# Keys and values dealt to partitions in pairs: the same loads in runs of 768 B instead of 1,536 B

## The chip, the cores and the metric

The kernel runs on one core of a Trainium2 chip. The metric is device time in microseconds (us) of one execution, lower is better. Five engines work beside each other and meet only through semaphores: TensorE (PE in the profile; PEld is its weight load), VectorE (DVE), ScalarE (ACT), GpSimd (POOL) and SyncE (SP). SP computes nothing here; it issues all DMAs, and 16 DMA engines carry them out.

## The reference

Attention over a cache of keys and values, with the projections of the queries and of the output. B = 8 batches, 112 queries each, D = 640; H = 32 heads of 192; 512 keys a head. Everything is bf16.

```python
q = transpose((x @ wq).reshape(B, Sq, H, Dh), 0, 2, 1, 3)
scores = einsum("bhqd,bhkd->bhqk", q, k_cache) * (Dh ** -0.5)
p = softmax(scores, axis=-1)
o = einsum("bhqk,bhkd->bhqd", p, v_cache)
return transpose(o, 0, 2, 1, 3).reshape(B, Sq, H * Dh) @ wo
```

The sum over the keys does not care in which order the 512 keys of a head stand, as long as keys, scores and values use the same order. That is the freedom which the change uses.

## The kernel before

**Tiling.** The 32 heads are four groups r of 8. A load i covers one group and one batch, r = i // 8, b = i % 8: K i and V i each hold 8 heads x 512 keys x 192, 1.573 MB. Each load serves two steps n = 2i and 2i + 1, with four heads each (`qd` = n % 2). For a step there are, in this order: the scores (`Sm`, `St`, L635 to L650), the softmax (`smax` on DVE L663, `exp` on ACT L668, `norm` on DVE L672), the transposes of p (`PT`, L706), and the value matmuls (`PVt` L739, `PVm` L750). Beside the steps run the query projection (`Q`, L590), which needs wq loads (`WQ`), and the output projection (`O`, L772), which needs wo loads (`WO`).

**How keys lie.** A head's 512 keys are dealt to 128 partitions, four neighbouring keys to each: partition r has keys 4r to 4r + 3, a run of 4 x 192 x 2 B = 1,536 B in memory. With q = 2a + e, a the pair and e the key in the pair, a run is (a, e, d). The 384 numbers of a pair make three blocks m of 128 after a transpose: block 0 is the first 128 of key e = 0, block 2 the last 128 of key e = 1, and block 1 holds the last 64 of the one and the first 64 of the other. A score bank therefore has 256 columns for a head and an e, those of a = 0 and a = 1; `QJ` = [0, 2, 1, 3] translates the order (e, a) of the score columns to the order (a, e) in which V's rows lie.

**How keys arrive.** The K loads 7 to 31 (`load_k`, L138) are transposing DMAs straight into `kt`, which has four buffers. The first seven loads (`load_kn`, L171, called KN 0 to 6; KN 0 in two halves) arrive plainly into borrowed space (`vt`, `wo_sb` or `accT` in the profile's names), are transposed by PE (`k_transposes`, L561) and moved to `kt` by ACT and DVE (L572). The values (`load_v`, L149) are plain loads into three buffers `vt`. At the end five p's (57 to 61) are transposed by DMA too (`TD`, L690).

**What sets the order.** Nothing is scheduled at run time. `ORDER_PE`, `ORDER_ACT`, `ORDER_DVE` and `ORDER_SP` are lists written out in the code, and every engine goes through its own list, waiting for semaphores. SP issues, in the order of `ORDER_SP`, a load as soon as the buffer is free (`deps`: for a K load the last score matmuls of the load four before, for a V load the last value matmuls of the load three before) and everything behind it in the list waits with it. Around the places that the prediction uses, the lists read:

```python
("K", 10), ("K", 9), ("V", 8), ("K", 11), ("WQ", 2, 0, 1), ("V", 9), ("V", 10), ...          # SP
("WQ", 3, 2, 1), ("V", 19), ("WQ", 3, 3, 1), ("WO", 2), ("V", 21), ("V", 22), ("K", 23), ...    # SP
("PT", 39, 5), ("Q", 6, 2, 0, 4), ("PVt", 38, 0), ("PVm", 38), ("PVt", 39, 5), ("Q", 6, 3, 0, 4), ("PVm", 39), ("S", 42),  # PE
```

Of the kernel before, what the change touches and what calls it, by code (L numbers as in the profile page):

```python
# [5 lines left out]
BF16 = mybir.dt.bfloat16  # L6
# [5 lines left out]
class Plan:  # L12
# [7 lines left out]
    def add(self, eng, name, deps, emit, sem=None, inc=1):  # L20
        assert name not in self.ops, name
        self.ops[name] = dict(eng=eng, deps=deps, emit=emit, sem=sem or eng, inc=inc)
# [30 lines left out]
def build_mha_kernel(nc, x, k_cache, v_cache, wq, wo, out):  # L53
    B, SQ, D = x.shape
# [3 lines left out]
    HU = 8  # L58
# [8 lines left out]
    KS, VS, QS = 4, 3, 2 * LP  # L67
# [18 lines left out]
    with ExitStack() as es:  # L86
        def sb(name, shape, dt):
            return es.enter_context(nc.sbuf_tensor(name, shape, dt))
# [2 lines left out]
        wo_sb = sb("wo_sb", [128, KB, D], BF16)  # L91
        accT = sb("accT", [128, 2, DC, SG], F32)
        xT_sb = sb("xT_sb", [128, DC, B * SQ], BF16)
        kt = sb("kt", [128, KS, 2, 3, HU * 128], BF16)
        vt = sb("vt", [128, VS, HU, 768], BF16)
        qr = sb("qr", [128, QS, 3, SG], BF16)
        qh = sb("qh", [128, 2, 2, 4, SQ], BF16)
# [9 lines left out]
        ps = es.enter_context(nc.psum_tensor("ps", [128, 8, 512], F32))  # L107
        psb = ps[:].bitcast(BF16)
# [4 lines left out]
        kn = [vt[:, VS - 1]]  # L113
# [5 lines left out]
        q_flat = qr[:].rearrange("p l c s -> p (l c s)")  # L119
        late = [wq_flat[:, i * 16 * SQ:(i + 1) * 16 * SQ] for i in range(4)] + [q_flat[:, 0:16 * SQ]]  # L120
        pT_late = dict(zip(BY_DMA, late))
        k3_flat = kt[:, KS - 1].rearrange("p a m c -> p (a m c)")
        zeros = k3_flat[:, 4 * D:4 * D + 256]
        xn = [k3_flat[:, 0:4 * D], acc_flat[:, 0:3 * D]]
        xn = [v.rearrange("p (c d) -> p c d", d=D) for v in xn]
# [7 lines left out]
        def load_k(i):  # L133
            r, b = divmod(i, B)
            name = ("K", i)

            def emit(e):
                src = k_cache[b, r * HU:(r + 1) * HU].rearrange("u (r q) d -> (u r) (q d)", q=4)  # L138
                return e.dma_start_transpose(kt[:, i % KS].rearrange("p a m c -> p (a m) c"), src)
            deps = [("St", 2 * (i - KS) + 1, 3)] if i >= KS else []  # L140
            if i == KS - 1:
                deps = [("XT", c) for c in range(4)]
            add("SP", name, deps, emit, f"mK{i % KS}", 16)

        def load_v(i):
            r, b = divmod(i, B)

            def emit(e):
                src = v_cache[b, r * HU:(r + 1) * HU].rearrange("u (r q) d -> r u (q d)", q=4)  # L149
                return e.dma_start(vt[:, i % VS], src)  # L150
            deps = [("PVm", 2 * (i - VS) + j, 1) for j in range(2)] if i >= VS else []
            if i == VS - 1:
                deps = [("KT", 0, p) for p in range(LP)]
            add("SP", ("V", i), deps, emit, f"mV{i % VS}", 16)
# [13 lines left out]
        def load_kn(i, lo, hi):  # L168

            def emit(e):  # L170
                return e.dma_start(kn[i][:, lo:hi, :], k_cache[i, lo:hi].rearrange("u (r q) d -> r u (q d)", q=4))  # L171
            old = [("KT", i - 2, p) for p in range(lo // 2, hi // 2)] if i > 2 else []
            add("SP", ("KN", i, lo, hi - lo), old, emit, f"mKN{i}_{lo}", 16)
            kn_of.update({(i, u): ("KN", i, lo, hi - lo) for u in range(lo, hi)})
# [382 lines left out]
        def k_transposes(i, p, bank, engs):  # L557
            def emit(e):
                for x in range(12):
                    c, u = divmod(x, 2)  # L560
                    ends = [e.transpose(psb[:, bank + t, x * 64:(x + 1) * 64],  # L561
                                        kn[i][64 * t:64 * t + 64, 2 * p + u, c * 128:(c + 1) * 128],
                                        ident[64 * t:64 * t + 64, 64 * t:64 * t + 64]) for t in range(2)]
                return tuple(ends)

            add("PE", ("KT", i, p), [kn_of[i, 2 * p], kn_of[i, 2 * p + 1]], emit, ("PE", "PE2"))
            old = [("St", 2 * (i - KS) + 1, 3)] if i >= KS else [("XT", x) for x in range(4)] if i == KS - 1 else []
            for t in range(2):
                def evac(e, t=t):
                    dst = kt[:, i % KS].rearrange("p a m (u t s) -> p (a m) u t s", t=2, s=64)[:, :, 2 * p:2 * p + 2, t, :]  # L570
                    src = psb[:, bank + t, 0:768].rearrange("p (c u s) -> p c u s", c=6, u=2)
                    return e.activation(dst, src, ACTF.Copy) if engs[t] == "ACT" else e.tensor_copy(dst, src)  # L572
                add(engs[t], ("evK", i, p, t), [("KT", i, p)] + old, evac)

# [27 lines left out]
        def q_of(n):  # L602

            r, b, qd = place(n)
            i, bb = q_slot(group(n), 2 * qd), b % (B // 2)
            return qr[:, i:i + 2, :, bb * SQ:(bb + 1) * SQ]
# [11 lines left out]
        def scores(n):  # L618
            qd = n % 2
            ktb = kt[:, n // 2 % KS]  # L620
            qv = q_of(n)

            def raw(j, c):
                return qv[:, j, c, :]

            def cs(i):
                return slice((4 * qd + i) * 128, (4 * qd + i + 1) * 128)

            for j in range(2):
                def emit(e, j=j):  # L630
                    for h in range(2):
                        i = 2 * j + h
                        ev, od = (raw(j, 0), qh[:, n % 2, j, 1, :]) if h == 0 else (qh[:, n % 2, j, 2, :], raw(j, 2))
                        hs = slice(h * 256, (h + 1) * 256)
                        e.matmul(ps[0:SQ, 2 * j, hs], ev, ktb[:, :, 0, cs(i)], start=(h == 0), stop=False,  # L635
                                 skip_group_check=True)
                        mm = e.matmul(ps[0:SQ, 2 * j + 1, hs], od, ktb[:, :, 2, cs(i)], start=(h == 0), stop=False,  # L637
                                      skip_group_check=True)
                    return mm
                add("PE", ("Sm", n, j), [("qc", n), ("smax", n - 1, 2 * j), ("smax", n - 1, 2 * j + 1)] +  # L640
                    ([("evK", n // 2, 2 * qd + i, t) for i in range(2) for t in range(2)] if n // 2 < NPL else [("K", n // 2)]), emit)
            for i in range(4):
                def emit(e, i=i):
                    j, h = divmod(i, 2)
                    ev, od = ((raw(j, 1)[0:64], qh[64:128, n % 2, j, 0, :]) if h == 0 else
                              (qh[0:64, n % 2, j, 3, :], raw(j, 1)[64:128]))
                    hs = slice(h * 256, (h + 1) * 256)
                    m1 = e.matmul(ps[0:SQ, 2 * j, hs], ev, ktb[0:64, :, 1, cs(i)], start=False, stop=True,  # L648
                                  skip_group_check=True)
                    m2 = e.matmul(ps[0:SQ, 2 * j + 1, hs], od, ktb[64:128, :, 1, cs(i)], start=False, stop=True,  # L650
                                  skip_group_check=True)
                    return m1, m2
                add("PE", ("St", n, i), [], emit, ("PE", "PE2"))
# [348 lines left out]
def bass_standalone__mha_block_cached__near_ridge_kernel(  # L1002
    nc: bass.Bass,
    x: bass.AP,
    k_cache: bass.AP,
    v_cache: bass.AP,
    wq: bass.AP,
    wo: bass.AP,
    out: bass.AP,
):  # L1010
    return build_mha_kernel(nc, x, k_cache, v_cache, wq, wo, out)
# [28 lines left out]
```

## Time and profile before

| | |
|---|---|
| median of 3 runs | 443.35 us (443.0 to 444.06) |
| profiled execution | span 444.4 us; no other time of it is given |
| granted TensorE clock, mean | 0.996 |
| busy | PE 96%, DVE 82%, ACT 78% of the span |
| DMA | 122.02 MB, mean 275 GB/s |
| V load, issue to landing | 9.0 us median, 32 of them |
| transposing K load, issue to landing | 10.2 us median, 25 of them |

The profile is that of one execution. A chain of work is followed back from the last instruction, at each step to what released it; its shares say which engine or transfer set the end. The window view gives busy time by engine, the granted clock, the mean busy share of the 16 DMA engines (over 1 where packets of one engine overlap) and what they moved. "Issue to landing" holds the time that a load stands behind others in the queue.

### The profile page before, as it was taken

The numbers are of one execution on the slowest core, as the hardware profiler recorded it, in microseconds if no ns is written. First come the engines' busy times: TensorE is split into PE (matmuls) and PEld (weight loads), VectorE is DVE, ScalarE is ACT, GpSimd is POOL, SyncE is SP. The second block draws the span as 40 slices with busy tenths as digits, with TensorE's granted clock in tenths as the row PEclk, the third lists the DMA queues.
The fourth block names the chain that finished last, engine by engine and source line by source line (L and its number), as shares of the span: only waits on it lengthen the run. The fifth ranks groups of instructions, "written<-read, shape, count | busy, mean of one in ns | idle before, by whom it ended". The sixth has DMA issues, their size and how long they took to land.

```text
span 444.4 us, 16108 instructions
## 1 busy us (share of the span) xinstructions
PE 425.1 (96%) x6805; PEld 304.5 (69%) x6805; DVE 363.2 (82%) x1165; ACT 344.4 (78%) x770; POOL 0.7 (0%) x6
## 2 busy tenths in 40 slices
PE   6998989889999999999899999999999999899995
PEld 4666666666677667777677766767667766676895
DVE  1579999879699889888989798889799888969871
ACT  3699999887678687978869688788778758965773
POOL 0000000000000000000000000000000000000000
PEclk9999999999999999999999999999999999989999
DMA  8999999998999999999999999999999999999952
GB/s 278 373 337 323 347 299 285 226 342 276 232 289 317 215 270 270 365 247 288 238 223 324 301 236 267 360 370 234 234 266 313 256 267 371 234 173 242 237 176 80
DMA packets 222184, 122.02 MB, mean 275 GB/s; under 512 B 164640, under 2 KB 222112, under 8 KB 222112
## 3 DMA queue, kind: packets, MB, share of 16 engines
q1 hardware_dynamic: 222112, 120.99, 106.6%
q8 instruction: 54, 0.88, 0.8%
q14 instruction: 18, 0.15, 0.1%
HBM read 78.22 MB, written 1.15 MB: 179 GB/s over the span
## 4 chain that ended last, share of the span: by engine, by line
PE 84%; DVE 5%; ACT 5%; DMA 4%; issue 2%; SPq 0%; ACTq 0%
PE ps L772 19%; PE ps L590 18%; PE ps L750 12%; PE ps L648 7%; PE ps L739 7%; PE ps L635 6%; PE ps L637 6%; PE ps L706 5%; DVE s_sb L663 3%; DMA wo_sb<-in_k_cache_dram 2%; PE ps L561 2%; ACT p_sb L668 2%; DMA wq_sb<-in_wq_dram 2%; ACT qr L595 1%; DVE p_sb L672 1%
## 5 line engine op out<-in xcount | busy, mean ns | idle before, releaser
L668 ACT ACTIVATE p_sb<-s_sb,nmx 112x512 bf16<-112x512 f32 x256 | 182.8, 717 | 31.6 <-DVE s_sb L663 26.8
L663 DVE TENSOR_SCALAR_CACHE_REDUCE s_sb<-ps 112x512 f32<-112x512 f32 x256 | 169.4, 684 | 29.6 <-PE ps L650 20.8
L590 PE MATMUL ps<-xT_sb,wq_sb 128*128 128x448 bf16 x480 | 102.0, 353 | 3.3 <-DMA wq_sb<-in_wq_dram 2.3
L772 PE MATMUL ps<-oT_sb,wo_sb 128*128 128x448 bf16 (+1 forms) x480 | 93.3, 341 | 0.1
L672 DVE TENSOR_SCALAR p_sb<-p_sb,rinv 112x512 bf16<-112x512 bf16 x256 | 81.3, 347 | 1.5
L590 PEld LDWEIGHTS ps<-xT_sb,wq_sb 128*128 128x128 bf16 x480 | 42.9, 98 | 41.5 <-DMA wq_sb<-in_wq_dram 2.9
L772 PEld LDWEIGHTS ps<-oT_sb,wo_sb 128*128 128x128 bf16 x480 | 44.3, 98 | 35.0 <-DVE pT_sb L719 0.5
L760 ACT ACTIVATE oT_sb<-ps 128x672 bf16<-128x672 f32 x64 | 46.3, 726 | 25.8 <-PE ps L750 25.4
L595 ACT ACTIVATE qr<-ps 128x448 bf16<-128x448 f32 x96 | 49.6, 539 | 12.7 <-PE ps L590 12.1
L750 PE MATMUL ps<-pT_sb,vt 128*128 128x112 bf16 x944 | 55.8, 215 | 2.0 <-issue 2.0
L719 ACT ACTIVATE pT_sb<-ps 128x768 bf16<-128x768 bf16 x59 | 47.0, 801 | 12.8 <-PE ps L706 12.8
L750 PEld LDWEIGHTS ps<-pT_sb,vt 128*128 128x128 bf16 x944 | 48.1, 99 | 6.3 <-issue 2.1
L668 ACT ACTIVATION_READ_ACCUMULATOR p_sb<-s_sb,nmx 112x1 f32 x256 | 49.5, 193 | 0.0
L719 DVE COPY pT_sb<-ps 128x1024 bf16<-128x1024 bf16 x59 | 40.3, 683 | 3.4 <-PE ps L706 2.6
L706 PE MATMUL ps<-ident,p_sb 64*128 64x64 bf16 (+1 forms) x1888 | 37.3, 185 | 1.2 <-issue 0.6
L706 PEld LDWEIGHTS ps<-ident,p_sb 64*128 64x128 bf16 (+1 forms) x1888 | 33.3, 94 | 5.8 <-DVE p_sb L672 2.0
L635 PE MATMUL ps<-kt,qr 128*112 128x256 bf16 x128 | 36.0, 282 | 0.9 <-ACT oT_sb L760 0.4
L637 PE MATMUL ps<-kt,qh 128*112 128x256 bf16 x128 | 35.2, 275 | 1.1 <-issue 1.1
L635 PE MATMUL ps<-kt,qh 128*112 128x256 bf16 x128 | 35.1, 274 | 0.0
L637 PE MATMUL ps<-kt,qr 128*112 128x256 bf16 x128 | 35.0, 274 | 0.0
L650 PE MATMUL ps<-kt,qh 64*112 64x256 bf16 x128 | 34.1, 291 | 0.1
L648 PE MATMUL ps<-kt,qr 64*112 64x256 bf16 x128 | 34.0, 291 | 0.0
(62 smaller groups left out, 478.6 us busy)
## 6 DMA issues: line engine op xcount, KB each, us to landing
vt<-in_v_cache_dram SPq DMA_DIRECT2D x32, 1536.0 KB, 9.0
wo_sb<-in_wo_dram SPq DMA_DIRECT2D x4, 1920.0 KB, 12.7
wq_sb<-in_wq_dram SPq DMA_DIRECT2D x14, 480.0 KB, 5.7
wo_sb<-in_k_cache_dram SPq DMA_DIRECT2D x3, 1536.0 KB, 9.3
accT<-in_k_cache_dram SPq DMA_DIRECT2D x3, 1536.0 KB, 12.7
vt<-in_k_cache_dram SPq DMA_DIRECT2D x2, 768.0 KB, 10.0
out_dram<-xT_sb SPq DMA_DIRECT2D x8, 140.0 KB, 3.2
wq_sb<-in_wq_dram SPq DMA_DIRECT2D x1, 960.0 KB, 10.6
```

The costliest lines, as they stand in the source:

```text
L590: mm = e.matmul(ps[:, bank, 0:SG], wq_sb[:, dc, c0:c0 + 128], xT_sb[:, dc, bh * SG:(bh + 1) * SG], start=(dc == 0), stop=(dc == DC - 1))
L595: return e.activation(qr[:, q_slot(g, lp), c, :], ps[:, bank, 0:SG], ACTF.Copy)
L635: e.matmul(ps[0:SQ, 2 * j, hs], ev, ktb[:, :, 0, cs(i)], start=(h == 0), stop=False, skip_group_check=True)
L637: mm = e.matmul(ps[0:SQ, 2 * j + 1, hs], od, ktb[:, :, 2, cs(i)], start=(h == 0), stop=False, skip_group_check=True)
L648: m1 = e.matmul(ps[0:SQ, 2 * j, hs], ev, ktb[0:64, :, 1, cs(i)], start=False, stop=True, skip_group_check=True)
L663: return e.tensor_scalar(s_sb[:, a, :].rearrange("p (e c) -> p e c", e=2), ps[0:SQ, 2 * j:2 * j + 2, h * 256:(h + 1) * 256], -scale, None, ...
L668: return e.activation(p_sb[:, k, :], s_sb[:, a, :], ACTF.Exp, bias=nmx[:, k:k + 1], scale=-1.0, accum_out=rsum[:, k:k + 1])
L672: return e.tensor_scalar(p_sb[:, k, :], p_sb[:, k, :], rinv[:, k:k + 1], None, op0=ALU.mult)
L706: ends.append(e.transpose(psb[:, bank + t, i * w:(i + 1) * w], p_sb[lo:hi, (4 * n + k) % 8, q * 128:(q + 1) * 128], ident[lo:hi, lo:hi]))
L719: return e.activation(dst, src, ACTF.Copy) if j == 0 else e.tensor_copy(dst, src)
L750: mm = e.matmul(ps[:, b0 + j, 2 * h * SQ:(2 * h + 1) * SQ], vtb[:, h0 + 2 * j + h, d0:d0 + 128], pT(j, h, q), start=(q == 0), stop=(q == 3))
L772: mm = e.matmul(ps[:, bank_of["O", g, m, 0], 0:nc_], wo_sb[:, k, m * 128:(m + 1) * 128], oT_sb[:, g % 2, k, 0:nc_], start=(k == 0), stop=( ...
```

## The change

A head's keys are dealt in pairs, not in fours: partition r has keys 2r and 2r + 1 (a = 0) and keys 256 + 2r and 257 + 2r (a = 1). Each pair is a run of 2 x 192 x 2 B = 768 B.

- The transposing loads read 2,048 rows of 384 numbers (8 heads x 256 pairs) instead of 1,024 rows of 768. `kt` becomes 3 blocks of 2,048 columns instead of 2 x 3 blocks of 1,024; the 256 columns of a head and an e now lie side by side.
- The plain loads of V and KN fetch two runs of 768 B for each partition and head, which land side by side where one run of 1,536 B landed.
- The transposes on PE take the same 24 blocks in another order, so that their evacuation can write the new layout; the score matmuls name one range of 256 columns instead of two of 128.

The instructions of each engine, their number, the lists and the waits stay.

```diff
-        kt = sb("kt", [128, KS, 2, 3, HU * 128], BF16)
+        kt = sb("kt", [128, KS, 3, HU * 256], BF16)
...
-        k3_flat = kt[:, KS - 1].rearrange("p a m c -> p (a m c)")
+        k3_flat = kt[:, KS - 1].rearrange("p m c -> p (m c)")
@@ load_k @@
-                src = k_cache[b, r * HU:(r + 1) * HU].rearrange("u (r q) d -> (u r) (q d)", q=4)
-                return e.dma_start_transpose(kt[:, i % KS].rearrange("p a m c -> p (a m) c"), src)
+                src = k_cache[b, r * HU:(r + 1) * HU].rearrange("u (c e) d -> (u c) (e d)", e=2)
+                return e.dma_start_transpose(kt[:, i % KS], src)
@@ load_v @@
-                src = v_cache[b, r * HU:(r + 1) * HU].rearrange("u (r q) d -> r u (q d)", q=4)
-                return e.dma_start(vt[:, i % VS], src)
+                src = v_cache[b, r * HU:(r + 1) * HU].rearrange("u (a r e) d -> r (u a) (e d)", a=2, e=2)
+                return e.dma_start(vt[:, i % VS].rearrange("p u (a c) -> p (u a) c", a=2), src)
@@ load_kn @@
-                return e.dma_start(kn[i][:, lo:hi, :], k_cache[i, lo:hi].rearrange("u (r q) d -> r u (q d)", q=4))
+                src = k_cache[i, lo:hi].rearrange("u (a r e) d -> r (u a) (e d)", a=2, e=2)
+                return e.dma_start(kn[i][:, lo:hi, :].rearrange("p u (a c) -> p (u a) c", a=2), src)
@@ k_transposes @@
-                    c, u = divmod(x, 2)
+                    m, u, a = x // 4, x // 2 % 2, x % 2
+                    c = 3 * a + m
...
-                    dst = kt[:, i % KS].rearrange("p a m (u t s) -> p (a m) u t s", t=2, s=64)[:, :, 2 * p:2 * p + 2, t, :]
-                    src = psb[:, bank + t, 0:768].rearrange("p (c u s) -> p c u s", c=6, u=2)
+                    dst = kt[:, i % KS].rearrange("p m (w t s) -> p m w t s", t=2, s=64)[:, :, 4 * p:4 * p + 4, t, :]
+                    src = psb[:, bank + t, 0:768].rearrange("p (m w s) -> p m w s", m=3, w=4)
@@ scores @@
-                return slice((4 * qd + i) * 128, (4 * qd + i + 1) * 128)
+                return slice((4 * qd + i) * 256, (4 * qd + i + 1) * 256)
...
-                        e.matmul(ps[0:SQ, 2 * j, hs], ev, ktb[:, :, 0, cs(i)], start=(h == 0), stop=False,
+                        e.matmul(ps[0:SQ, 2 * j, hs], ev, ktb[:, 0, cs(i)], start=(h == 0), stop=False,
```

The other three score matmuls (L637, L648, L650) change in the same way, with blocks 2, 1 and 1.

More of the change, by code (lines that the diff above doesn't have):

```diff
@@ L634, in emit @@
                         hs = slice(h * 256, (h + 1) * 256)
-                        e.matmul(ps[0:SQ, 2 * j, hs], ev, ktb[:, :, 0, cs(i)], start=(h == 0), stop=False,
+                        e.matmul(ps[0:SQ, 2 * j, hs], ev, ktb[:, 0, cs(i)], start=(h == 0), stop=False,
                                  skip_group_check=True)
-                        mm = e.matmul(ps[0:SQ, 2 * j + 1, hs], od, ktb[:, :, 2, cs(i)], start=(h == 0), stop=False,
+                        mm = e.matmul(ps[0:SQ, 2 * j + 1, hs], od, ktb[:, 2, cs(i)], start=(h == 0), stop=False,
                                       skip_group_check=True)
@@ L647, in emit @@
                     hs = slice(h * 256, (h + 1) * 256)
-                    m1 = e.matmul(ps[0:SQ, 2 * j, hs], ev, ktb[0:64, :, 1, cs(i)], start=False, stop=True,
+                    m1 = e.matmul(ps[0:SQ, 2 * j, hs], ev, ktb[0:64, 1, cs(i)], start=False, stop=True,
                                   skip_group_check=True)
-                    m2 = e.matmul(ps[0:SQ, 2 * j + 1, hs], od, ktb[64:128, :, 1, cs(i)], start=False, stop=True,
+                    m2 = e.matmul(ps[0:SQ, 2 * j + 1, hs], od, ktb[64:128, 1, cs(i)], start=False, stop=True,
                                   skip_group_check=True)
```

## The prediction
> **What bounds the kernel now.** I read the first parts of the page, then the waits, then stretches of the window view, then the DMA queue's own timeline against the chain.
>
> ```profile
> span 444.4 us, 16108 instructions
> ...
> PE 425.1 (96%) x6805; PEld 304.5 (69%) x6805; DVE 363.2 (82%) x1165; ACT 344.4 (78%) x770; POOL 0.7 (0%) x6
> DMA  8999999998999999999999999999999999999952
> DMA packets 222184, 122.02 MB, mean 275 GB/s; under 512 B 164640, under 2 KB 222112, under 8 KB 222112
> ...
> PE 84%; DVE 5%; ACT 5%; DMA 4%; issue 2%; SPq 0%; ACTq 0%
> ```
>
> PE is busy 425.1 of 444.4 us and holds 84% of the chain. But the DMA digits read 9 nearly throughout too: two resources are full, and the change touches the second. DMA has only 4% of the chain, so the first question is who waits for it.
>
> ```profile
> PE ps L590 <- DMA wq_sb<-in_wq_dram: 2.3, 2, 2.0
> ...
> PE ps L561 <- DMA wo_sb<-in_k_cache_dram: 1.4, 1, 1.4
> ...
> 33.96 9.34 DMA wo_sb<-in_k_cache_dram
> ```
>
> These are all of PE's waits for DMA that the waits view names: two at the start for Q weights, which stand in the queue ahead of every changed load, and one of 1.4 us for a changed load, the key load KN 3, issued at 33.96 and landed 9.34 us later. No row has PE waiting for a V load or for a transposing K load. So today the changed loads cost PE 1.4 us. The next view (window, PE, PEld, DVE, ACT and POOL busy with counts, clock, DMA share, GB/s) tells how much room is left.
>
> ```profile
> 109.00:109.40 0.40, 0.40 (x3) 0.20 (x3) 0.37 (x3) 0.00 (x0) 0.00 (x0) 1.00 0.00 0
> 109.40:174.00 64.60, 64.60 (x931) 44.95 (x930) 55.69 (x178) 47.63 (x109) 0.00 (x0) 1.00 1.18 259
> 174.00:239.00 65.00, 63.60 (x998) 45.29 (x996) 57.69 (x188) 53.82 (x126) 0.00 (x0) 1.00 1.17 276
> 239.00:290.00 51.00, 50.99 (x799) 36.09 (x798) 43.53 (x143) 40.44 (x93) 0.00 (x0) 1.00 1.14 302
> 290.00:345.00 55.00, 54.72 (x833) 38.34 (x832) 47.93 (x160) 45.07 (x105) 0.00 (x0) 1.00 1.15 282
> ```
>
> The queue is empty at 109.0 to 109.4 (0 GB/s). From there to 345 its share stays above 1.1 (packets of one engine overlap), while PE is busy for 233.9 of 235.6 us. I read that as a backlog that never drains: what one load takes longer is handed to the next, and adds up until a load is late for PE. SP does wait for PE before many issues, but issues into a backlog, so those waits do not take the lateness back.
>
> **How much lateness fits.** Counts between the dry point and the tightest loads, from the lines of the V and K issues in the window 108 to 278, then the three tight loads with their landing, then PE's arrival on the chain.
>
> ```profile
> L150 SPq DMA_DIRECT2D vt<-in_v_cache_dram x13: 367/527/985, 122.0 to 277.4; - x13
> ...
> L139 SPq DMA_TRANSPOSE kt<-in_k_cache_dram x14: 6109/7038/14037, 108.6 to 262.4; - x14
> ...
> L150 SPq DMA_DIRECT2D vt<-in_v_cache_dram x1: 522/522/522, 277.4 to 277.4; - x1
> DMA to landing us min/median/max: 9.4/9.4/9.4
> ...
> L193 SPq DMA_DIRECT2D wo_sb<-in_wo_dram x1: 2352/2352/2352, 279.0 to 279.0; - x1
> DMA to landing us min/median/max: 14.7/14.7/14.7
> ...
> L150 SPq DMA_DIRECT2D vt<-in_v_cache_dram x1: 582/582/582, 327.5 to 327.5; - x1
> DMA to landing us min/median/max: 11.6/11.6/11.6
> ```
>
> ```profile
> 287.29 0.51 PE ps L739 x16
> ...
> 294.02 2.27 PE ps L772 x12
> ...
> 340.21 0.52 PE ps L739 x16
> ```
>
> The load at 277.4 is V 19, the 13th V after the dry point. It lands at 277.4 + 9.4 = 286.8; its first reader, PVt 38, runs on the chain from 287.29: slack 0.5. WO 2 lands at 279.0 + 14.7 = 293.7 and O 4 starts at 294.02: slack 0.3, with the same 13 V ahead of it. V 23 lands at 327.5 + 11.6 = 339.1 for PVt 46 at 340.21: slack 1.1, the 17th V after the dry point (21, 22, 24 and 23 follow V 19 in SP's list). If a V takes d longer and a K takes k longer, PE is late by the largest, not the sum, of 13d + 14k - 0.5, 13d + 14k - 0.3 and 17d + 18k - 1.1.
>
> **The change part by part.** *Plain loads (32 V, 7 KN).* The bytes are the same; 1,024 runs of 1,536 B become 2,048 of 768 B for a load of 1.573 MB. The trace holds 768 B runs already: the WQ loads (two heads of 192 columns by 2 B). Windows in which one kind of load streams alone:
>
> ```profile
> 126.00:129.00 3.00, 3.00 (x94) 2.69 (x91) 2.73 (x8) 2.08 (x5) 0.00 (x0) 1.00 1.06 374
> 30.50:32.50 2.00, 2.00 (x65) 1.34 (x58) 1.74 (x6) 2.00 (x5) 0.00 (x0) 1.00 1.06 376
> 174.00:175.20 1.20, 1.20 (x43) 0.95 (x40) 0.96 (x4) 1.20 (x5) 0.00 (x0) 1.00 1.09 363
> 273.50:274.50 1.00, 1.00 (x6) 0.38 (x4) 1.00 (x5) 0.85 (x3) 0.00 (x0) 1.00 1.08 361
> 55.00:56.00 1.00, 0.47 (x25) 0.35 (x19) 1.00 (x4) 1.00 (x2) 0.00 (x0) 1.00 1.09 357
> ...
> 29.00:30.00 1.00, 1.00 (x6) 0.41 (x5) 0.97 (x4) 1.00 (x4) 0.00 (x0) 1.00 1.06 396
> 3.00:4.00 1.00, 1.00 (x7) 0.74 (x6) 0.00 (x0) 0.00 (x0) 0.00 (x0) 1.00 1.06 392
> ```
>
> The first two are V (mean 375 GB/s: 4.19 us a load), the next three WQ (mean 360: 4.37 us). So d = 0.18 us, 4%. Bounds: against the best V window (29 to 30: 396 GB/s, 3.97 us) the same 360 gives d = 0.40; on the other side, runs of 1,280 B (the x load, 3 to 4) went at 392, so shorter than 1,536 B is not slower in itself, and at that rate d = -0.18. I take 0.18, from like windows in mid-kernel.
>
> The Trainium skill speaks against the change here: "DMA: Bandwidth & Descriptors", section "Why small descriptors are slow (HBM only)", has a fixed cost of about 3 cycles a packet beside one cycle for 32 B. Estimated from that page, 48 + 3 = 51 cycles become 2 x (24 + 3) = 54, 5.9%, which would be d = 0.25 and 2.9 us late at WO 2. The trace's windows say 4%, so it agrees in sign and roughly in size.
>
> *Transposing loads (25 K).* The source is read as 2,048 rows of 768 B instead of 1,024 of 1,536 B; 3 groups of 128 columns instead of 6. The packets do not change: of 164,640 below 512 B, the five p transposes (L690) have 112 rows x 16 groups each, 8,960 in all; 25 x 1,024 x 6 = 153,600 are K's, 256 B each; the last 2,080 are 16 completions for each of 130 ends of transfers. After, 2,048 x 3 is again 6,144 a load. Two K windows and, as the nearest other source, one of a p transpose with rows of 4,096 B:
>
> ```profile
> 129.50:132.50 3.00, 3.00 (x57) 2.26 (x55) 2.89 (x13) 3.00 (x8) 0.00 (x0) 1.00 1.27 290
> 118.50:122.50 4.00, 4.00 (x45) 2.49 (x38) 2.03 (x7) 3.53 (x8) 0.00 (x0) 1.00 1.28 290
> 402.60:404.40 1.80, 1.80 (x11) 0.89 (x10) 1.75 (x6) 1.38 (x4) 0.00 (x0) 1.00 1.10 207
> ```
>
> Different keys, the same 290 to the digit: this looks like a rate of 256 B packets, not of the memory behind them. I take k = 0. Above: at 207 GB/s a load's streaming grows from 5.42 to 7.60 us, k = 2.2. Below, nothing excludes a gain from denser rows. Because k is multiplied by 14 to 18, this is the term that could swamp the rest.
>
> *Engines.* One answer for all of it, nothing: the transposes of KN are the same 24 per pair in another order; the evacuation still moves 128x768 in runs of 64; score matmuls still take 256 columns, now in one run instead of two of 128, and are already issued 0.11 us apart, as the chain has them (one row of many):
>
> ```profile
> 277.90 0.11 PE ps L635
> ```
>
> QJ, softmax and the value matmuls find the keys in the same (e, a, r) order. No wait is added, removed or moved on SP.
>
> **The sum.** At the start KN 3 is waited for directly and nothing hides it: +0.18. Later 13 x 0.18 - 0.5 = 1.8 at V 19; 13 x 0.18 - 0.3 = 2.0 at WO 2, of which V 19 has paid 1.8; 17 x 0.18 - 1.1 = 2.0 at V 23, already paid. Sum 0.2 + 2.0 = 2.2 us on a span of 444.4. No time of the profiled execution is known but its span, which lies 1.05 us above the median of the runs, 443.35; I put the difference on the median: 445.6 us.
>
> **The rivals.**
> 1. *The forecast:* plain loads cost a little each and the backlog adds it up. With d from 0.08 to 0.40: at the low end 0.1 + 0.7 = 0.8, at the high end 0.4 + 5.7 = 6.1 us; 444.2 to 449.5. For it: full DMA digits, the three tight loads. Against it: the slack could grow if bubbles between loads shrink. Chance 0.57.
> 2. *The transposes slow down* with the other pitch. Price 14 us for each us of k at V 19; at half the bound, k = 1.1, 18 x 1.1 + 2.0 = 21.8 us more, 465; at k = 0.3, 5.4 + 2.2: 451. For it: a different source gave 207. Against it: packets unchanged, a constant 290. Chance 0.16.
> 3. *Nothing to measure:* 768 B runs stream like 1,536 B ones. By the rows, d below 0.03 (0.4 us over 13 loads) never reaches PE, and the result is 443.4. For it: 356 to 363 against 374 to 376 are close, in short windows. The rule of "DMA: Bandwidth & Descriptors", section "Specifications", that 512 B is enough for line rate, would give this; the trace's 4% speaks mildly against it. Chance 0.17.
> 4. *The other side, not slower:* denser rows and half as many column groups speed up the K transposes. It decides from k = -0.15 on: 14 x 0.15 = 2.1 us undo all that 13 V add before WO 2. PE then gains nothing more from K, since it never waits for K; what can still be won is the 1.4 us at KN 3, if the runs of 768 B also go at 392 GB/s or better: 0.2 us of it at 392, all 1.4 only if the load is that much quicker. So 441.9 to 443.2, 442.6 at the middle. For it: nothing measured here, only that the bound is open below. Chance 0.10.
>
> **How the numbers follow.** About 0.2%, 0.9 us, is what a measurement of this kernel can tell from no change. Slower by more: cases 1 and 2, 0.73. Within: case 3, 0.17. Faster: case 4, 0.10. The time is case 1's, 445.6. The range goes from 442.9, in the upper part of case 4, through case 3 and all of case 1, to 453.0, where case 2 has k near 0.4; left out are most of case 2 and half of case 4, about 0.2. Case 1's own range is 444.2 to 449.5.
>
> **What would show it.** Right: packets of 1,536 B gone, so some 40,000 packets more and the same number under 512 B; V windows at about 360 GB/s; K windows still at 290; PE's waits gain rows for DMA vt or wo_sb near 287 to 294, of 1.5 to 2 us together. Wrong: K windows off 290 (case 2 or 4), V windows at 375 (case 3), or PE's extra idle time lying somewhere else than at a V or WO load, on DVE or ACT for instance.

## The result and the profile after

The change makes the kernel slower: median 459.2 us of 4 runs (457.74 to 461.31) against 443.18 of 4 runs of the kernel before beside them (442.64 to 444.06), ratio 1.0341 [1.0284, 1.0397] (the two medians by themselves give 1.036; the costs below go by the ratios). The forecast was 445.6 us with a range to 453.0: the direction was right, the size not, and the result lies outside the range. The profiled execution has a span of 458.1 us, 13.7 more than before. From its page:

```profile
span 458.1 us, 16108 instructions
...
PE 428.2 (93%) x6805; PEld 305.3 (67%) x6805; DVE 363.4 (79%) x1165; ACT 344.5 (75%) x770; POOL 0.7 (0%) x6
...
DMA  8999999999999999999999999999999999999972
...
DMA packets 262119, 122.00 MB, mean 266 GB/s; under 512 B 164640, under 2 KB 262048, under 8 KB 262048
...
PE 75%; DMA 10%; ACT 6%; DVE 6%; issue 2%; SPq 1%; ACTq 0%; DVEq 0%
```

The same 16,108 instructions; DVE and ACT are as busy as before to 0.2 us, PE 3.1 us longer. There are 39,935 packets more and the same 164,640 below 512 B. DMA's share of the chain went from 4% to 10%. The waits view names what PE now waits for:

```profile
PE ps L592 <- DMA wq_sb<-in_wq_dram: 5.7, 4, 2.9
...
PE ps L741 <- DMA vt<-in_v_cache_dram: 2.8, 1, 2.8
```

A V load is waited for (L741 is L739 of before), and WQ loads four times instead of twice; the wait for KN 3 is still there, 1.3 us. To see where PE falls behind, the chain of both kernels at the same instructions (start, duration, group); of before first:

```profile
102.79 1.24 PE ps L772 x6
...
224.49 1.02 PE ps L739 x32
...
249.80 0.91 PE ps L739 x32
...
273.36 1.24 PE ps L772 x6
...
351.97 0.91 PE ps L739 x32
...
432.96 0.91 PE ps L739 x32
```

and of after, with the two loads that the chain names:

```profile
34.38 10.46 DMA wo_sb<-in_k_cache_dram
...
107.14 1.24 PE ps L774 x6
...
227.56 1.05 PE ps L741 x32
...
255.84 0.98 PE ps L741 x32
...
279.47 1.24 PE ps L774 x6
...
288.99 12.07 DMA vt<-in_v_cache_dram
301.20 0.96 PE ps L741 x16
...
310.20 2.27 PE ps L774 x12
...
368.14 0.91 PE ps L741 x32
...
447.90 0.91 PE ps L741 x32
```

Row by row, after minus before. KN 3 lands at 44.84 instead of 43.30: 1.5 us late. At 107 PE is 4.4 us late, at 227 still 3.1, at 256 6.0, at 279 6.1. Then V 19, issued at 288.99, lands at 301.06, and its reader starts 13.9 us late (301.20 against 287.29); O 4 starts 16.2 us late (310.20 against 294.02). The lateness is the same 16.2 at 368 and 14.9 near the end. So most of the loss is made between 227 and 310 us, at V and WO loads of the long backlog that began at 109 us. That is the forecast's place, but 13.1 us instead of 2.0. The rates say why (window, five engines, clock, DMA share, GB/s; a window with V loads, then one with K):

```profile
256.00:262.00 6.00, 6.00 (x121) 4.92 (x117) 2.48 (x8) 3.18 (x7) 0.00 (x0) 1.00 1.09 326
265.50:269.50 4.00, 4.00 (x57) 2.52 (x57) 3.68 (x12) 2.91 (x7) 0.00 (x0) 1.00 1.28 290
```

V loads stream at 326 GB/s, not at the forecast's 360. The transposing K loads keep their 290 to the digit.

### The profile page after: what moved, and what is told of

Same layout as the page of the kernel before. It is cut to its first block, busy times and chain, and to the rows that moved or that the text cites. A ratio compares the mean times of both kernels' runs of the same rounds, so it can differ in the third digit from the quotient of the medians.

```text
span 458.1 us, 16108 instructions
## 1 busy us (share of the span) xinstructions
PE 428.2 (93%) x6805; PEld 305.3 (67%) x6805; DVE 363.4 (79%) x1165; ACT 344.5 (75%) x770; POOL 0.7 (0%) x6
## 2 busy tenths in 40 slices
DMA packets 262119, 122.00 MB, mean 266 GB/s; under 512 B 164640, under 2 KB 262048, under 8 KB 262048
## 4 chain that ended last, share of the span: by engine, by line
PE 75%; DMA 10%; ACT 6%; DVE 6%; issue 2%; SPq 1%; ACTq 0%; DVEq 0%
PE ps L592 17%; PE ps L774 15%; PE ps L752 11%; PE ps L650 7%; PE ps L741 6%; PE ps L637 6%; PE ps L639 5%; PE ps L708 5%; DVE s_sb L665 4%; ACT p_sb L670 3%; DMA vt<-in_v_cache_dram 3%; DMA wq_sb<-in_wq_dram 3%; DMA wq_sb<-p_sb 2%; DMA wo_sb<-in_k_cache_dram 2%; PE ps L563 2%
## 5 line engine op out<-in xcount | busy, mean ns | idle before, releaser
L592 PE MATMUL ps<-xT_sb,wq_sb 128*128 128x448 bf16 x480 | 103.7, 358 | 7.0 <-DMA wq_sb<-in_wq_dram 5.7
L741 PE MATMUL ps<-pT_sb,vt 128*64 128x112 bf16 x944 | 33.3, 218 | 5.9 <-DMA vt<-in_v_cache_dram 2.8
L637 PE MATMUL ps<-kt,qr 128*112 128x256 bf16 x128 | 35.8, 280 | 2.9 <-DVE s_sb L665 2.3
L682 DVE RECIPROCAL rinv<-rsum 112x2 f32<-112x2 f32 x128 | 19.4, 159 | 22.4 <-ACT p_sb L670 21.8
L741 PEld LDWEIGHTS ps<-pT_sb,vt 128*64 128x64 bf16 x944 | 26.0, 112 | 16.4 <-issue 7.0
L639 PE MATMUL ps<-kt,qh 128*112 128x256 bf16 x128 | 34.9, 273 | 0.0
```

Source lines behind the costliest of these rows:

```text
L592: mm = e.matmul(ps[:, bank, 0:SG], wq_sb[:, dc, c0:c0 + 128], xT_sb[:, dc, bh * SG:(bh + 1) * SG], start=(dc == 0), stop=(dc == DC - 1))
L637: e.matmul(ps[0:SQ, 2 * j, hs], ev, ktb[:, 0, cs(i)], start=(h == 0), stop=False, skip_group_check=True)
L639: mm = e.matmul(ps[0:SQ, 2 * j + 1, hs], od, ktb[:, 2, cs(i)], start=(h == 0), stop=False, skip_group_check=True)
L741: mm = e.matmul(ps[64 * h:64 * h + 64, b0 + j, SQ:2 * SQ], vtb[:, h0 + 2 * j + h, d0:d0 + 64], pT(j, h, q), start=(q == 0), stop=(q == 3))
```

## The experiments

Theory P, from the two traces: a plain load of 768 B runs in a backlog takes 1.573 / 326 = 4.82 us instead of 4.19, so d is 0.63, not 0.18, and the backlog adds it up. Rival K: the transposing loads, or the new layout of `kt` on PE, cost the time. The first four kernels share the runs of the kernel before (445.31 us median; their ratios are against these).

**Only the plain loads changed** (before, with after's V and KN loads; the K loads, `kt` and the scores as before).

```diff
@@ before: load_v (and load_kn in the same way) @@
-                src = v_cache[b, r * HU:(r + 1) * HU].rearrange("u (r q) d -> r u (q d)", q=4)
-                return e.dma_start(vt[:, i % VS], src)
+                src = v_cache[b, r * HU:(r + 1) * HU].rearrange("u (a r e) d -> r (u a) (e d)", a=2, e=2)
+                return e.dma_start(vt[:, i % VS].rearrange("p u (a c) -> p (u a) c", a=2), src)
...
```

> The kernel before with the plain loads (V and KN) of the changed kernel; the K transposes, kt and the score matmuls stay as before (keys and values are then dealt differently, so the result is another one; nothing else is left out). Theory P (the plain loads are the cause; in a backlog a V of 768 B runs takes 4.8 us, not 4.2): nearly all of the loss, 455 to 460 us. Rival K (the transposes with the other pitch take a good part of it, about 0.3 us each): 448 to 451.

460.97 us, ratio 1.0326 [1.0265, 1.0387], nearly the whole loss, and 1 us above the top of theory P's 455 to 460. Three V loads, V 16, V 19 and V 23, stand on its chain, where before had none:

```profile
247.23 8.91 DMA vt<-in_v_cache_dram
...
289.17 11.96 DMA vt<-in_v_cache_dram
...
343.00 12.92 DMA vt<-in_v_cache_dram
```

**Only the other half** (after's K loads, `kt`, transposes and scores; V and KN in runs of 1,536 B).

```diff
@@ after: load_v (and load_kn in the same way) @@
-                src = v_cache[b, r * HU:(r + 1) * HU].rearrange("u (a r e) d -> r (u a) (e d)", a=2, e=2)
-                return e.dma_start(vt[:, i % VS].rearrange("p u (a c) -> p (u a) c", a=2), src)
+                src = v_cache[b, r * HU:(r + 1) * HU].rearrange("u (r q) d -> r u (q d)", q=4)
+                return e.dma_start(vt[:, i % VS], src)
...
```

> The other half: kt, K transposes, evacuation and score matmuls of the changed kernel, V and KN loads in runs of 1,536 B as before (again keys and values are dealt differently). Theory P: 442.5 to 444, no change. Rival K: 447 to 450; if denser rows help the transposes, 441 to 442.5.

444.14 us, ratio 0.9973 [0.9934, 1.0012], as theory P expected (442.5 to 444, at its upper end): the transposing loads of 768 B rows, the new layout and the one-range score matmuls cost nothing that can be measured. Rival K falls, and with it the prediction's second rival.

**V alone, and KN alone**, the same edits separately.

> The kernel before with only the V loads of the changed kernel (KN as before, keys and values dealt differently). Theory P: the part after 109 us, 13 x 0.63 - 0.3 = 8 us and whatever PE's slower clock after a stall adds: 451 to 455. Rival K: 445 to 448.

> The kernel before with only the seven KN loads of the changed kernel. Theory P: the early part alone, 1.5 us at KN 3 and up to 4.4 by 109 us: 444.5 to 447.5, with V landing as before. Rival K: 443.5 to 444.5.

V alone: 457.59 us, ratio 1.0252 [1.0181, 1.0324], above the 451 to 455 that was expected. KN alone: 447.14, ratio 1.0039 [1.0003, 1.0076], inside its expectation of 444.5 to 447.5. Of the 14.5 us that both together cost in the first kernel (3.26% of 445.31), 11.2 are V's and 1.7 KN's; the sum, 12.9, falls short of 14.5 by less than the intervals.

**Is it the backlog?** If d only counts because nothing takes lateness back, two loads fewer early in the backlog must give time back at V 19, far behind them, and d in eight loads alone must make V 19 late. Rival L: each late load is late for a reason of its own place. The first of the next two kernels leaves out the loads V 9 and V 10 of after.

```diff
@@ after @@
-                load_v(*a)
+                load_v(*a) if a[0] not in (9, 10) else None
...
-        order["SP"] = ORDER_SP
+        order["SP"] = [o for o in ORDER_SP if o not in (("V", 9), ("V", 10))]
```

> The changed kernel with the loads V 9 and V 10 left out (steps 18 to 21 use the values that lie in the buffers). Both had 20 to 27 us to spare in the changed kernel. Theory B (backlog: what PE loses near V 16 to V 19 is the sum over all loads since the queue was last empty): 2 x 4.8 = 9.6 us less in the queue, so nearly everything lost after 109 us comes back, 446 to 451 us. Rival L (each late load is late for its own longer transfer): these two were never late, so nothing changes, 457 to 461.

The median is 454.85 us (450.51 to 456.6), ratio 1.0203 [1.0151, 1.0255] against 444.7 of the runs beside it; its profiled execution has a span of 448.5. Between 105 and 260 us PE now waits for nothing: the wait for V 16, which after has (it is read further below), is gone. V 19 is still waited for. From the waits view, the lines of V 19's issue and landing, and the chain:

```profile
PE ps L741 <- DVE p_sb L674: 2.3, 1, 2.3
...
L150 SPq DMA_DIRECT2D vt<-in_v_cache_dram x1: 1410/1410/1410, 279.2 to 279.2; - x1
...
DMA to landing us min/median/max: 11.5/11.5/11.5
...
290.79 0.61 PE ps L741 x16
```

The view puts the wait down to DVE, but V 19 lands at 279.2 + 11.5 = 290.7 and its reader starts 0.1 us later, so I read it as V 19's. What counts is the landing: 290.7 instead of the 301.1 of after, 10.4 us earlier, although the two loads left out stand some 150 us ahead of V 19. That speaks for the backlog and against L. The median lies between the two expectations: of the 9.6 us of transfer left out (two loads of 4.82), (1.0341 - 1.0203) x 444 = 6.1 came back. The profiled execution, the quickest of the four, lies the whole 9.6 us below that of after (448.5, 458.1); of these, 1.9 us were there before the loads left out, since K 10 was issued at 111.09 instead of 112.96. The rest of the difference from the median is open.

The second changes V 8 to V 15 alone, on before.

```diff
@@ before: load_v @@
+                if 8 <= i <= 15:
+                    src = v_cache[b, r * HU:(r + 1) * HU].rearrange("u (a r e) d -> r (u a) (e d)", a=2, e=2)
+                    return e.dma_start(vt[:, i % VS].rearrange("p u (a c) -> p (u a) c", a=2), src)
```

> The kernel before in which only the loads V 8 to V 15 come in the changed kernel's runs of 768 B (their keys and values are dealt differently); all eight have 8 to 29 us to spare before. Theory B: 8 x 0.63 - 0.3 = 4.7 us, paid at V 19 and WO 2, and up to 3 us more if PE's clock halves after the stall: 447 to 451. Rival L: no change, 442.5 to 444.

451.67 us, ratio 1.0141 [1.0106, 1.0177], 0.7 us above the expectation of the backlog (447 to 451), far from L's 442.5 to 444. V 19, itself unchanged, is the load that the chain stops at; ahead of it, V 16's reader:

```profile
250.03 0.91 PE ps L742 x32
...
279.41 13.08 DMA vt<-in_v_cache_dram
```

V 19 is issued at 279.41 and lands at 292.5 instead of 286.8. PE was not the carrier: at V 16's reader it was 0.2 us late (250.03 against 249.80), and it waits for nothing between 105 and 285 us. So what V 8 to 15 took longer was handed on by the loads themselves, past V 16, 17 and 18. Not all of the 5.7 us are theirs: K 10, ahead of them, already landed 1.4 us late in this execution. The same count for the other kernels, in us of landing later than before (K 10 lands at 118.7 and V 19 at 286.8 before):

| kernel | K 10 | V 19 | made between | V loads changed between, x 0.63 |
|---|---|---|---|---|
| after | 4.6 | 14.3 | 9.7 | 13: 8.2 |
| V and KN changed | 4.1 | 14.3 | 10.2 | 13: 8.2 |
| V alone | 2.7 | 11.1 | 8.4 | 13: 8.2 |
| V 8 to 15 alone | 1.4 | 5.7 | 4.3 | 8: 5.0 |
| after without V 9, V 10 | 2.7 | 3.9 | 1.2 | 11, two loads fewer |

The lateness made on the way follows the number of changed loads to within 2 us. The two loads left out took 8.5 us of it away (9.7 - 1.2), of the 9.6 expected.

**The rates by themselves.** A kernel with nothing but loads: single loads of 1.573 MB, then six in a row, in runs of 3,072, 1,536 and 768 B; then transposing loads from rows of both lengths (repeated calls are written as loops here).

```python
plain(e, S[2], 2, 768, 0); e.wait_ge(S[2], 16)              # single
for j in range(6): plain(e, S[6], 16 + j, 768, j)           # six in a row
for j in range(4): tr(e, S[9], 4 + j, 2, j)                 # transposing, rows of 2 keys (768 B)
```

> No attention at all, output zeros: plain loads of 1.573 MB each with runs of 3,072, 1,536, 768 and 384 B, one alone and six behind each other, then four K transposes with rows of 1,536 B and four with rows of 768 B; no other engine works. Theory Q (a queue with more than one load in it costs some 4 ns a packet more, whatever the size): the first load of a burst at about 395 GB/s with 1,536 B and 365 with 768, the later ones at 375 and 326. Rival E (the engines' own traffic slows the packets in the kernel): all loads at 395 and 365, in bursts too. Transposes: 290 GB/s with both rows by theory P.

Its windows (DVE, POOL, clock, share, GB/s): single loads of 3,072, 1,536 and 768 B runs; later in six of 3,072, 1,536 and 768 B; transposes from rows of 1,536 and of 768 B.

```profile
6.00:9.00 3.00, 0.00 (x0) 0.00 (x0) 1.00 1.03 420
```

```profile
13.00:15.00 2.00, 0.00 (x0) 0.00 (x0) 1.00 1.06 401
19.00:21.00 2.00, 0.00 (x0) 0.00 (x0) 1.00 1.08 361
...
41.00:55.00 14.00, 0.00 (x0) 0.00 (x0) 1.00 1.03 402
64.00:83.00 19.00, 0.00 (x0) 0.00 (x0) 1.00 1.06 373
91.00:114.00 23.00, 0.00 (x0) 0.00 (x0) 1.00 1.10 326
162.00:166.00 4.00, 0.00 (x0) 0.00 (x0) 1.00 1.28 290
189.00:192.00 3.00, 0.00 (x0) 0.00 (x0) 1.00 1.28 290
```

With no engine at work the rates of the kernel come out again: 326 for 768 B and 373 for 1,536 B in a row, 401 and 361 in the first part of a load alone (the window of 361 reaches past that part; the next kernel has 373 and 365 within it), 290 for transposes from either row. So the V rate is the transfers' own, and no contention with the engines. (A fourth size, 384 B, reached the chip as packets of 1,536 B and tells nothing.)

**Whose state is it?** Loads alone again, all in 768 B runs unless said: four that each wait until the one before has landed; twelve half loads in a row; six issued in turn from SP's and ACT's queues; six of 1,536 B from both queues. The first calls of the first three:

```python
plain(e, S[0], 0, 768, 0); e.wait_ge(S[0], 16)              # single, four times
half(e, S[4], 4, 0, 0); half(e, S[4], 4, 1, 0)              # half loads, twelve
plain(sync, S[5], 10, 768, 0); plain(scalar, S[5], 11, 768, 1)   # from two queues, six
```

> Loads alone, no attention is computed and the output is zeros; its time by itself means nothing, the rates do. Four stretches: four loads of 1.573 MB in 768 B runs, each issued when the one before has landed; twelve half loads in 768 B runs back to back on one queue; six loads in 768 B runs issued in turn from two queues (SP and ACT); six loads in 1,536 B runs from the two queues. Theory Q (one queue's own state: once some 1,100 to 1,400 packets have gone without a pause, a packet takes 41 ns instead of 36, or 69 instead of 65): single loads run at about 360 GB/s and fall to 326 only in their last part; the half loads reach 326 after two or three of them; each of two queues has its own state, so 768 B runs from two queues reach 326 later or, when they share the engines in turn, stay near 326 in the end, and 1,536 B runs near 373. Rival E (the cost belongs to the issue of loads, a later load's issue disturbing the earlier one): single loads stay at 360 to their end, and half loads, with twice the issues, fall below 326. Rival M (the memory side limits long bursts): two queues change nothing at all, and single loads with pauses of about 2 us between them are again at 360 from their start.

Windows: near the end of a single load; the half loads; two queues with 768 B; two queues with 1,536 B.

```profile
8.80:9.60 0.80, 0.00 (x0) 0.00 (x0) 1.00 1.10 326
...
39.00:63.00 24.00, 0.00 (x0) 0.00 (x0) 1.00 1.10 327
69.00:92.00 23.00, 0.00 (x0) 0.00 (x0) 1.00 1.09 326
102.00:121.00 19.00, 0.00 (x0) 0.00 (x0) 1.00 1.06 373
```

A load alone falls to 326 before its own end, so no later issue is needed for it, and twice the issues change nothing: rival E falls. The quick first part comes back in each single load after a pause of less than 2 us. Two queues share the same 326 or 373, so the state is not one queue's own, as Q had it first; rival M and Q's second form (the engines taken in turn) both expected this and are not told apart. In these two kernels the rate falls some 3 to 6 us after the first packet behind a pause; what sets that point, the runs do not show.

**Keys in pairs, V and KN in fours, the orders matched** (the kernel of the other half, and the softmax's first pass reads the score bank with step 2 from load 7 on, so that its order is V's).

```diff
@@ after: the scores' smax (and load_v, load_kn as in the other half) @@
-                    return e.tensor_scalar(s_sb[:, a, :].rearrange("p (e c) -> p e c", e=2),
-                                           ps[0:SQ, 2 * j:2 * j + 2, h * 256:(h + 1) * 256], -scale, None,
+                    dst = s_sb[:, a, :].rearrange("p (e c) -> p e c", e=2)
+                    src = ps[0:SQ, 2 * j:2 * j + 2, h * 256:(h + 1) * 256]
+                    if n // 2 >= NPL:
+                        dst = dst.rearrange("p e (a r) -> p e a r", a=2)
+                        src = src.rearrange("p e (r a) -> p e a r", a=2)
+                    return e.tensor_scalar(dst, src, -scale, None,
```

> A version that computes the reference: K transposes in pairs (768 B rows) as changed, V and KN in runs of 1,536 B as before; the order of the keys is put right by smax, which reads the score bank with a step of 2 columns from load 7 on. Theory P: as the half e2, 0.995 to 1.0 of the time before, if the stepped read costs DVE nothing; with 0.1 us more for each of 200 smax it would be slower by 1 to 5 us. Rival K is out of this by e2.

445.12 us, ratio 0.9989 [0.9959, 1.002], as expected: the half of the change that costs nothing brings nothing either. No version beats the kernel before.

## Why the prediction was right and wrong

*What bounds the kernel: right in what it does, not in how it was read.* From 109 us on the loads hand lateness on, and V 19 and WO 2 were the place; V 8 to 15 alone made V 19 late. But the DMA share above 1.1 is a mean over 51 to 65 us. It hides that the queue all but stands still between many loads, as the short windows below show (8 GB/s at 123.5 to 124.5). So it is no backlog that never drains; what the landings show is that these gaps take little lateness back: in after, from K 10 (4.6 us late) to V 19 (14.3 us late) no load lands more than 2.1 us less late than the load ahead of it.

*The terms that failed: d, and the start.* Two terms of the sum were sized wrong: d, 0.18 where 0.63 was measured, and what PE is late when the backlog begins, 0.18 where 4.4 was measured. First d. It was sized from V windows (374, 376) against WQ windows (363, 361, 357), as "like windows in mid-kernel". They were not alike. Before, just ahead of the first two WQ windows, then ahead of the first V window's load and at its start:

```profile
172.50:173.00 0.50, 0.50 (x11) 0.50 (x7) 0.50 (x2) 0.15 (x1) 0.00 (x0) 1.00 0.48 63
271.50:272.00 0.50, 0.50 (x7) 0.50 (x6) 0.00 (x0) 0.50 (x3) 0.00 (x0) 1.00 0.76 109
123.50:124.50 1.00, 1.00 (x7) 0.49 (x5) 0.79 (x4) 0.58 (x2) 0.00 (x0) 1.00 0.07 8
125.00:125.50 0.50, 0.50 (x7) 0.50 (x5) 0.50 (x2) 0.46 (x1) 0.00 (x0) 1.00 1.09 304
```

At 63 and 109 GB/s the queue had all but run dry: I read these WQ windows as the quick start after a pause. The V load of 125 has a gap close ahead of it too, but inside the tail of K 9, whose last packets it follows at once, and no quick start; why that gap does not count, the runs do not show. That the rate is not a matter of the kind of load, two WQ loads show that the change does not touch. Behind K 22 they streamed at 361 in before (the window at 273.5); behind K 22 in after they have the rate of a row:

```profile
285.50:287.00 1.50, 0.58 (x32) 0.46 (x32) 1.47 (x6) 0.79 (x1) 0.00 (x0) 1.00 1.10 326
```

Like with like, by the kernel of loads alone: after a pause 401 against 361, in a row 373 against 326. Mixed, 373 against 361, 3%, close to the prediction's 4%. By a row of plain loads d = 1.573/326 - 1.573/373 = 0.61 us; from the kernel's own windows, 375 and 326, 0.63. The upper bound of 0.40 compared 396 with 360: like with like, but both after a pause, and so no bound for loads in a row. At 373 and 326 GB/s, 16 engines start a packet every 65.9 and 37.7 ns each, so 768 B more cost 28.2 ns and the fixed part of a packet is 9.5 ns, 8 times what 32 B take. The rule of the Trainium skill, "DMA: Bandwidth & Descriptors", section "Why small descriptors are slow (HBM only)", has the same form with a smaller fixed cost, about 3 cycles a packet beside one cycle for 32 B. The rule of the same page of the Trainium skill, section "Specifications", that 512 B is enough for line rate, is contradicted: 768 B runs give 326 where 3,072 B runs give 402.

*The formula.* With d = 0.63 it gives 13 x 0.63 - 0.5 = 7.7 at V 19. Measured is 13.9. It left out that PE may be late already when the backlog begins: SP issues a load when PE has freed its buffer, and K 10, the first after the dry point, was issued at 112.96 instead of 108.6, as late as PE is at 107. 4.4 + 8.2 - 0.5 = 12.1 of 13.9; the last 1.8 us are not assigned. Nor was V 19 the first to bind. V 16 was, which is not among the prediction's tight loads: before, it landed 5.8 us ahead of its reader. In after (its issue and landing, then PE's wait in the window 252 to 257):

```profile
L150 SPq DMA_DIRECT2D vt<-in_v_cache_dram x1: 575/575/575, 247.2 to 247.2; - x1
...
DMA to landing us min/median/max: 8.5/8.5/8.5
```

```profile
PE ps L741 <- DVE s_sb L665: 2.4, 1, 2.4
```

It lands at 255.7 and its first reader, waiting for 2.4 us, starts at 255.84. The view puts the wait down to DVE, whose last record came within 0.1 us of that; before, the same reader started at 249.80 right behind PE's previous work, so I read it as V 16's. The first kernel, with the plain loads alone, bears that out. There V 16, issued at 247.23, is the load on the chain, and the wait at the same reader (window 252 to 258) is put down to it:

```profile
PE ps L740 <- DMA vt<-in_v_cache_dram: 3.2, 1, 3.2
```

*The start: +0.18 was wrong in kind.* KN 3 was taken as one load with one d. But KN 0 to 2, V 2 and V 0 stand ahead of it: the start has a backlog too, and KN 3 is 1.5 us late (43.30 to 44.84). Of the other 2.9 of the 4.4 us at 107 us, 1.8 are rows "issue" of the chain, holes in which PE waits for nothing that the profile shows: up to 107 us after has 3.8 us of them (four, at 50.60, 70.44, 77.12 and 91.95) and before 2.0 (two, at 80.68 and 94.51). What they are stays open. The change may have a part in them: up to 110 us they come to 3.7 to 4.1 us in the four kernels whose early V loads are changed, and to 0.8 to 2.3 in the other five kernels that compute the attention, one execution each. Over the whole chain it is 3.8 against 5.0 in before, which has two more at 220.61 and 387.28; that is why PE's lateness falls to 3.1 behind the one and from 16.2 to 14.9 behind the other. So by this count they move the lateness about and are no part of the loss as a whole.

*The transposes: right.* k = 0: 290 GB/s in the K windows before and after, and shown apart by the second kernel and by the loads alone. *The engines: right,* nothing. *Rivals:* 2 and 4 (K slower, K quicker) fall with k = 0; 3 (nothing to measure) falls with d. *The range* failed with the bound on d: at 0.63 its own case 1 reads 17 x 0.63 - 1.1 + 0.63 = 10.2, 453.6, just outside 453.0; most of the rest is the early lateness, which the formula had no term for.

## What to carry to other kernels

Compare transfer rates only between windows in the same place of a queue: the head of an empty queue and the middle of a backlog differ by nearly as much as the two run lengths do. Long windows do not show whether a queue runs dry; short ones, and the landings of load after load, do. Where loads hand lateness on for 200 us, size a change of every load per load and times the number of loads ahead of the tightest one, and add what the consumer is late already at the point where that begins. Here runs of 768 B stream 1.08 to 1.11 times slower than runs of 1,536 B after a pause (373 to 361 against 401), and 373 / 326 = 1.14 times in a row.

## What the hardware showed beyond that

A packet takes longer once loads have streamed without a pause for a few us, by nearly the same time whatever its size: from share and rate of the windows above, 16 x 768 x 1.08 / 361 = 36.8 ns after a pause and 16 x 768 x 1.10 / 326 = 41.5 in a row; for 1,536 B 65.0 and 69.8; for 3,072 B 120.5 and 125.9. Some 5 ns for each packet, so short runs pay it more often.

The second concerns PE's clock. In after, from 295.9 us on, within PE's 2.9 us wait for a WQ load and through the wait for V 19 that follows, the granted clock was half for 10.2 us, three times 3.4 (after, then before):

```profile
295.90:306.10 10.20, 6.95 (x58) 4.17 (x59) 2.32 (x9) 2.67 (x6) 0.00 (x0) 0.50 1.08 345
```

```profile
389.00:393.50 4.50, 4.26 (x46) 3.85 (x48) 1.28 (x6) 2.30 (x5) 0.00 (x0) 0.62 1.26 284
```

Before has one such stretch, of 3.4 us ((1 - 0.62) x 2 x 4.5), behind the hole of 1.96 us in PE's issue at 387.28; after has neither there. So a late load costs more than its wait: between V 19's reader at 301.20 and 306.1 PE ran 4.9 us at half clock, which is 2.5 us of work lost, and O 4 was 2.3 us later than V 19's reader (16.2 against 13.9). The Trainium skill, "TensorE: Matmul & The Clock Gate", Part 1, has the clock halved after an idle window of about 3.4 us. The lengths here agree with that window, though no wait of PE that the views of these two executions name was longer than 2.9 us.
